# Turning finished attention segments on VectorE in 32x32 blocks, with output projections on the mixed layout

## The chip, the cores and the metric

The kernel runs on one core of a Trainium2 chip. The core has TensorE (PE in the profile; its weight loads are listed as PEld), VectorE (DVE), ScalarE (ACT), GpSimd (POOL) and SyncE (SP, which here only issues transfers), each with an instruction stream of its own; they wait for each other by semaphores. SBUF is the working memory of 128 partitions, PSUM holds the results of TensorE in eight banks of 128 x 512 fp32. The metric is the device time of one execution in microseconds.

## The reference, cut to what matters

Four layers over x of 2048 tokens and 512 features, alternating two kinds, each on the layer-normed input and added back to x:

```python
def _A_ref(x, wq, wk, wv, wo):            # layers 0 and 2
    H = 32; Dh = 16                       # 32 query heads, one shared key and value head
    q = (x @ wq).reshape(B, S, H, Dh) ... # to heads first
    k = x @ wk; v = x @ wv
    p = softmax(einsum("bhqd,bkd->bhqk", q, k) * Dh ** -0.5)
    o = einsum("bhqk,bkd->bhqd", p, v)
    return o.reshape(B, S, H * Dh) @ wo

def _B_ref(x, wqkv, wo):                  # layers 1 and 3: linear attention
    q, k, v = ...; phi = lambda t: where(t > 0, t + 1, exp(t)) + 1e-6
    kv = einsum("bhsd,bhse->bhde", phi(k), v); z = phi(k) summed over s
    o = (phi(q) @ kv) / (phi(q) . z + 1e-6)
    return o.reshape(B, S, D) @ wo

x = x + _A_ref(_layernorm(x), ...); x = x + _B_ref(_layernorm(x), ...)   # twice
```

## The kernel before, in words

The 2048 tokens are 16 tiles of 128. A Python planner (class `Planner`) plays the whole program through with a list of assumed durations, gives each operation to an engine when it is eligible, the engine free and its priority first, and writes down the order. The instruction streams are those orders, fixed when the program is built; the assumed durations (0.6 for a copy of 128x512, 0.12 for a transpose, ...) thus decide the order, though not the real time.

**Attention (layers 0 and 2, `run_a`).** A segment (`Seg`) is one query tile and one parity of heads: QT holds the queries of a tile as 128 partitions (four groups j of 32, two heads each) by four groups of 128 tokens, and the masked key array KM picks even or odd heads. A block is one key tile and one j: a score matmul with 32 rows (L1051) gives 128 keys x 512 columns in a PSUM bank. The exponential of a block is done by ScalarE for two or three banks at once (L1240, from `act_stream`), or by VectorE (L1344): it writes int16 bits, and GpSimd adds constants to four such blocks as 64-bit integers three times (L1386) to make three weighted shifts of it, so that a block done by VectorE is multiplied by the values four times (VW) instead of once (V). The results lie in W, 72 blocks of SBUF. `pv_try` sends value matmuls (L1105) in fours, one for each j, 32 columns wide, side by side in the array, all into bank 6 (ACC). Six banks hold scores; bank 7, and at times others, serve everything else from the pool `banks`. When TensorE would idle, `fill` adds matmuls with zero weights (L1150).

**The end of a segment.** `norms` takes the segments in turn. When all value matmuls of one are sent, VectorE copies ACC to SBUF as fp32 (`sacc`, L1407), which frees ACC for the next segment. Segments of the first tiles come in two or three parts over the keys; the first part is copied, later ones are added to it (L1409), and only the last is normalized. `norm` then acquires a bank, turns sacc by four fp32 transposes on TensorE (L1429), takes the reciprocal of the denominators, which are column 16 of each 32 (L1436), and multiplies (L1440) into Osb in bf16: tokens on partitions, features in the order of the heads.

**The output projection (`epilogue`).** Both parities done, Osb is turned to OT by a transposing DMA on SP (L794, tiles below 12), or by TensorE (L1468; L815 for tile 15). Four full matmuls with OT as weights and wo as moving data (L786) go to a bank, which VectorE adds to x (L1486). Tile 15, which ends the stage, goes through `proj2` (L829, L837) in two halves of 256 columns with x added by TensorE, followed at once by the next layer's statistics.

**Linear attention (layers 1 and 3, `run_b`)** is worked off beside the attention as far as its tiles are ready: projections (L786, L966), `phi` (ScalarE L1516, VectorE L1517 and L1519), sums over tokens. L1517 and the layer norm's scaling (L884) read and write SBUF only; the planner keeps them and GpSimd's L1386 apart in its own time (`port=True`). L936 makes the weighted values VW.

**Weights.** `late` loads wo, wqkv and wo2 on SP's queue once the keys of layer 0 are there.

Of the kernel before, what the change touches and what calls it, by code (L numbers as in the profile page):

```python
# [16 lines left out]
P = 128  # L17
# [533 lines left out]
def bass_interleave_layers__grouped_kv_mqa__linear_attn_block__prompt_kernel(  # L551
# [11 lines left out]
    pl = Planner(nc)  # L563
# [142 lines left out]
    def late():  # L706
        yield ("flag", ("K", 0, T - 1))
        pool_op(lambda e: e.memset(va[:].rearrange("p t (h c) -> p (t h) c", c=17)[:, :, DH:DH + 1], 1.0), [("va", i) for i in range(8)], dur=1.2, prio=5.0)
        dma(wo[:], A_wo.rearrange("(g r) c -> r g c", r=P), ["wo"], 3.0, 4.5)
        dma(wqkv[:], B_wqkv.rearrange("(ft f) c -> f ft c", f=P), ["wqkv"], 3.1, 9.5)  # L710
        dma(wo2[:], B_wo.rearrange("(g r) c -> r g c", r=P), ["wo2"], 3.2, 10.5)

# [110 lines left out]
        b1 = yield ("acq", banks, prio)  # L823
        return b0, b1

    def proj2(bs, lhs, rhs, t, key, prio):
# [4 lines left out]
        for h in range(2):  # L831
            hs = slice(h * 256, h * 256 + 256)

            def fn(e, h=h, hs=hs):
                ins = None
                for g in range(4):
                    ins = e.matmul(bank(bs[h], 256), lhsT=lhs(g), rhs=rhs(g, hs), start=False, stop=(g == 3))  # L837
                return ins
            op({PE: (0.45, fn)}, reads=key, writes=[B_(bs[h])], prio=prio, lat=0.2).cols = 1024
        os_ = []  # L840
        for h in range(2):
            hs = slice(h * 256, h * 256 + 256)
# [199 lines left out]
    def run_a(L):  # L1042
# [353 lines left out]
        def norms():  # L1396
            for sg in segs:
                pl.flag(("acc", L, sg.i))
                pl.at(pl.now, pv_kick)
                yield ("flag", ("pv", L, sg.i))  # L1400
                if sg.first and sg.last:
                    a_ = yield ("acq", as_pool, 0.0)
                    src, key = sacc[:, a_, :], ("sacc", a_)
                else:
                    a_, src, key = None, sacc[:, sg.unit, :], ("sacc", sg.unit)
                if sg.first:
                    o = op({DV: (0.6, lambda e, src=src: e.tensor_copy(src, bank(ACC)))}, writes=[B_(ACC), key], prio=0.0, lat=0.15)  # L1407
                else:
                    o = op({DV: (0.6, lambda e, src=src: e.tensor_tensor(out=src, in0=src, in1=bank(ACC), op=ALU.add))},  # L1409
                           writes=[B_(ACC), key], prio=0.0, lat=0.15)  # L1410
                if sg.last:
                    pl.process(norm(sg, src, key, a_))
                yield ("ops", [o])
            lin["a"] = False
            if L == 2 and LEND:
                lin["lent"] = True
                plain_give(banks, ACC)

        def norm(sg, src, key, a_):
            pr = 0.5  # L1420
            if sg.par == 0:
                oslot[sg.t] = yield ("acq", os_pool, 0.0)
                pl.flag(("oslot", L, sg.t))
            yield ("flag", ("oslot", L, sg.t))
            yield from until(key)
            b = yield ("acq", banks, pr)

            for c in range(4):
                o = op({PE: (0.12, lambda e, c=c: e.transpose(ps[:, b * 512 + c * P:b * 512 + (c + 1) * P], src[:, c * P:(c + 1) * P], identF[:]))},  # L1429
                       reads=[key, "identF"], writes=[B_(b)], prio=pr, lat=0.2)  # L1430
# [4 lines left out]
            rr = rden[:, r_, :].rearrange("p (c j) -> p c j", j=4)  # L1435
            op({DV: (0.17, lambda e: e.reciprocal(rr.unsqueeze(3), v4[:, :, :, DH:DH + 1]))},  # L1436
               writes=[B_(b), ("rden", r_)], prio=pr, lat=0.15)
            dst = Osb[:, oslot[sg.t], :].rearrange("p (g j r d) -> p r g j d", g=4, j=4, r=2)[:, sg.par]
            rb = rr.unsqueeze(3).to_broadcast([P, 4, 4, DH])
            o = op({DV: (0.33, lambda e: e.tensor_tensor(out=dst, in0=v4[:, :, :, 0:DH], in1=rb, op=ALU.mult))},  # L1440
                   reads=[("rden", r_)], writes=[B_(b), ("Osb", oslot[sg.t], sg.par)], prio=pr, lat=0.15)
            pl.give_after(banks, b, [o])
            yield ("ops", [o])
            pl.flag(("O", L, sg.t, sg.par))

        def epilogue(t):
# [29 lines left out]
                yield from until(("OT", m))  # L1476
            if t in ECRIT:
                bs = yield from acq2(pr)
                proj2(bs, lambda g: OT[:, m, g, :], lambda g, hs: wo[:, g, hs], t, [("OT", m), "wo"], pr)
# [499 lines left out]
```

## Time and profile before

| | |
|---|---|
| median of three timed runs | 1393.38 us (1393.33 to 1393.57) |
| profiled execution, its own time | 1391.23 us |
| its span | 1389.3 us |
| granted TensorE clock, mean | 0.999 |
| busy: TensorE, ScalarE, VectorE, GpSimd | 1344.2, 1347.3, 1216.5, 1033.0 us |
| exponentials on ScalarE (L1240) | 1332 instructions, 1287.5 us |
| exponentials on VectorE (L1344) | 1332 blocks, 868.8 us |
| copies of ACC (L1407) | 64, 43.6 us |
| transposes of sacc on TensorE (L1429) | 256, 46.0 us |
| scaling into Osb (L1440) | 64, 26.7 us |

How to read it: a row of a group names the source line, the engine, the operation, what it writes and reads by the program's names, the shapes and the count; then the busy time and the mean duration of one; then the idle time of the engine just before and what ended it. A wait row names the waiting engine and line, whom it waited for, the total, how often, the longest. A row of a stretch of time has the busy time of each engine with its instruction count, then the granted clock and the transfers. A timeline row has the start, the length, the engine and the operation. TensorE's busy time includes overlapped matmuls and filler, so its share alone says little.

### The profile page before, as it was taken

Reading aid. Unit: us, or ns where it says so; the run is one execution under the profiler, and the core shown is the slowest. Engines: PE = TensorE matmul, PEld = TensorE weight load, DVE = VectorE, ACT = ScalarE, POOL = GpSimd, SP = SyncE. Lnnn points to the kernel's source line nnn. Section 1 sums busy time; section 2 is a strip of 40 time slices with the busy share of each in tenths; the row PEclk is TensorE's granted clock in tenths of the full one; section 3 lists DMA queues with packets and bytes.
Section 4 is the critical chain, followed back from the end, with each engine's and each line's share of the span. In section 5 each row is a group of like instructions: output and inputs, shape, how many; then the busy total and the mean of one; then the engine's idle time right before and its main releaser. Section 6 shows DMA issues by size and latency. Waiting matters only on the chain.

```text
span 1389.3 us, 38426 instructions
## 1 busy us (share of the span) xinstructions
PE 1344.2 (97%) x15092; PEld 465.4 (33%) x15092; DVE 1216.5 (88%) x2184; ACT 1347.3 (97%) x1543; POOL 1033.0 (74%) x1031
## 2 busy tenths in 40 slices
PE   8999999999999999999999999999999999999998
PEld 5422222232222222233632333333333322223335
DVE  8889888898889988897889988988898899888977
ACT  8999999999999999999799999999999999999996
POOL 1489998778979998776005878867888799977770
PEclk9999999999999999999999999999999999999999
DMA  4300000000000000000021000000000000000001
GB/s 108 93 6 5 6 6 20 6 13 2 10 9 6 5 6 13 2 1 3 5 51 36 5 5 9 21 6 6 13 6 9 5 6 5 6 13 2 2 2 62
DMA packets 52465, 20.58 MB, mean 15 GB/s; under 512 B 46144, under 2 KB 51776, under 8 KB 52288
## 3 DMA queue, kind: packets, MB, share of 16 engines
q1 hardware_dynamic: 51232, 18.10, 5.7%
q8 instruction: 122, 2.00, 0.6%
q14 instruction: 55, 0.45, 0.1%
q10 hardware_dynamic: 1056, 0.03, 0.0%
HBM read 5.28 MB, written 2.10 MB: 5 GB/s over the span
## 4 chain that ended last, share of the span: by engine, by line
PE 52%; ACT 29%; DVE 9%; issue 7%; POOL 1%; DMA 1%; SPq 0%; ACTq 0%; DVEq 0%; POOLq 0%
ACT W L1240 28%; PE ps L1105 20%; PE ps L1051 17%; PE ps L786 6%; DVE W L1344 5%; PE ps L966 3%; PE ps L1429 2%; PE ps L1150 2%; POOL W L1386 1%; ACT phE L1516 1%; DVE phE L1517 1%; DVE sacc L1407 1%; DVE xn L884 1%; DMA x_sb<-in_A_x_dram 1%; DVE st L871 0%
## 5 line engine op out<-in xcount | busy, mean ns | idle before, releaser
L1240 ACT ACTIVATE W<-ps 128x1024 bf16<-128x1024 f32 (+1 forms) x1332 | 1287.5, 1157 | 11.5 <-PE ps L1051 8.4
L1386 POOL INT64_ADD W<-W x999 | 1027.4, 1041 | 314.7 <-DVE W L1344 156.8
L1344 DVE TENSOR_SCALAR W<-ps 128x512 int16<-128x512 f32 x1332 | 868.8, 683 | 121.8 <-PE ps L1051 106.5
L1105 PE MATMUL ps<-W,VW 128*32 128x512 bf16 x5328 | 562.4, 384 | 7.5 <-DVE sacc L1407 7.1
L1051 PE MATMUL ps<-QT,KM 32*128 32x512 bf16 x4096 | 520.7, 385 | 23.9 <-ACT W L1240 12.9
L1105 PE MATMUL ps<-W,V 128*32 128x512 bf16 x2764 | 447.7, 384 | 0.0
L1051 PEld LDWEIGHTS ps<-QT,KM 32*128 32x128 bf16 x4096 | 130.5, 91 | 508.0 <-ACT W L1240 444.6
L1105 PEld LDWEIGHTS ps<-W,VW 128*32 128x32 bf16 x5328 | 133.7, 94 | 177.6 <-issue 115.8
L1105 PEld LDWEIGHTS ps<-W,V 128*32 128x32 bf16 x2764 | 108.0, 94 | 71.2 <-issue 46.7
L786 PE MATMUL ps<-wqkv,xnT 128*128 128x512 bf16 (+1 forms) x272 | 76.1, 371 | 1.7 <-DVE sacc L1519 1.5
L1150 PE MATMUL ps<-QT,V 128*32 128x512 bf16 (+4 forms) x278 | 74.1, 333 | 0.9 <-DVE QT L780 0.8
L1516 ACT ACTIVATE phE<-ps 128x512 bf16<-128x512 f32 (+1 forms) x66 | 43.5, 663 | 6.8 <-PE ps L966 6.7
L1407 DVE COPY sacc<-ps 128x512 f32<-128x512 f32 x64 | 43.6, 681 | 6.0 <-PE ps L1105 5.9
L1429 PE MATMUL ps<-identF,sacc 128*128 128x128 f32 x256 | 46.0, 292 | 1.6 <-DVE sacc L1519 0.8
L871 DVE BATCH_NORM_STATS2 st<-x_sb 128x6 f32<-128x512 bf16 x60 | 40.5, 680 | 0.6 <-DMA x_sb<-in_A_x_dram 0.3
L884 DVE TENSOR_SCALAR xn<-x_sb,mv,rs 128x512 bf16<-128x512 bf16 x64 | 35.6, 571 | 2.2 <-ACT rs L862 2.0
L966 PE MATMUL ps<-xnT,wqkv 128*128 128x128 bf16 x512 | 37.4, 220 | 0.0
L1517 DVE TENSOR_SCALAR phE<-phE 128x512 bf16<-128x512 bf16 (+1 forms) x66 | 33.2, 506 | 4.5 <-ACT phE L1516 4.1
L786 PE MATMUL ps<-wo,OT 128*128 128x512 bf16 x120 | 36.0, 384 | 0.9 <-DVE QT L1519 0.5
L966 PE MATMUL ps<-xnT,wq 128*128 128x128 bf16 x464 | 35.2, 220 | 0.0
L1429 PEld LDWEIGHTS ps<-identF,sacc 128*128 128x128 f32 x256 | 27.6, 142 | 19.9 <-issue 14.3
L1150 PEld LDWEIGHTS ps<-QT,V 128*32 128x32 bf16 x278 | 22.7, 95 | 29.7 <-issue 15.6
(140 smaller groups left out, 599.0 us busy)
## 6 DMA issues: line engine op xcount, KB each, us to landing
out_dram<-x_sb SPq DMA_DIRECT2D x16, 128.0 KB, 1.7
x_sb<-in_A_x_dram SPq DMA_DIRECT2D x6, 256.0 KB, 5.4
wqkv<-in_B_wqkv_dram SPq DMA_DIRECT2D x1, 1536.0 KB, 7.9
xnT<-xn SPq DMA_TRANSPOSE x46, 2.5
x_sb<-in_A_x_dram SPq DMA_DIRECT2D x4, 128.0 KB, 2.2
wq<-in_A_wq_dram SPq DMA_DIRECT2D x1, 512.0 KB, 4.2
wo<-in_A_wo_dram SPq DMA_DIRECT2D x1, 512.0 KB, 4.1
wo<-in_B_wo_dram SPq DMA_DIRECT2D x1, 512.0 KB, 8.8
```

Of the source, the lines that this page charges most:

```text
L786: return e.matmul(dst, lhsT=l, rhs=r, start=(k == 0), stop=(k == len(pairs) - 1))
L884: op({DV: (0.325, lambda e: e.tensor_scalar(out=xn[:, i, :], in0=x_sb[:, t, :], scalar1=mv[:, t, 0:1], scalar2=rs[:, t:t + 1], op0=ALU.sub ...
L966: ins = e.matmul(dst[:, g * P:(g + 1) * P], lhsT=lhs(g, k), rhs=rhs(k), start=(k == 0), stop=(k == FT - 1))
L1051: return e.matmul(bank(b), lhsT=KM[r, sg.par, kt * P:(kt + 1) * P], rhs=QT[r, sg.t, :], start=True, stop=True)
L1105: ins = e.matmul(ps[32 * j:32 * j + 32, ACC * 512:(ACC + 1) * 512], lhsT=V[:, kt, :] if w is None else VW[:, kt, w, :], rhs=ap, start=(k = ...
L1150: o = op({PE: (n / 2400.0, lambda e: e.matmul(ps[32 * j:32 * j + 32, b * 512:b * 512 + n], lhsT=V0[:], rhs=QT[:, sg.t, 0:n], start=st, sto ...
L1240: ex = op({AC: (EXO + 0.4267 * n, lambda e, n=n, s_=s_, p_=p_: e.activation(ws_(p_), ps[:, s_ * 512:(s_ + n) * 512], ACTF.Exp, scale=EXPSC ...
L1344: o = op({DV: (0.602, lambda e: e.tensor_scalar(out=dst.bitcast(I16), in0=bank(b), scalar1=VB, scalar2=VLO, op0=ALU.add, op1=ALU.max))}, w ...
L1386: o = op({PO: (512 * m * PSR + PSO, lambda e, g_=g_, f_=f_: e.int64_add(ws_(g_).bitcast(I64), ws_(f_).bitcast(I64), step))}, reads=wk_(f_) ...
L1407: o = op({DV: (0.6, lambda e, src=src: e.tensor_copy(src, bank(ACC)))}, writes=[B_(ACC), key], prio=0.0, lat=0.15)
L1429: o = op({PE: (0.12, lambda e, c=c: e.transpose(ps[:, b * 512 + c * P:b * 512 + (c + 1) * P], src[:, c * P:(c + 1) * P], identF[:]))}, rea ...
L1516: op({AC: (0.07 + n / 1200.0, lambda e: e.activation(phE[:, i, 0:n], bank(b, n), ACTF.Exp))}, reads=[B_(b)], writes=[("phE", i)], prio=pr ...
```

## The change

VectorE has a transpose that turns each 32x32 block of a 128x512 array on its own. A segment that comes in one part is turned by it straight out of ACC into sacc, in place of the copy; one that comes in parts is copied and added as before, and its sum is turned from SBUF into one of the two `as_pool` slots of sacc. TensorE's transposes and the bank they needed go. The result has a mixed layout: on partition 32j + q lies token q of each of the four 32-token blocks b of a tile, for the heads of group j. Reciprocal and scaling read it in SBUF, and Osb has its columns ordered by b, then by head within j. After the same transposing step as before, OT holds for each b the features of all four j side by side, 32 columns for each j. The output projection therefore takes, for each j, four matmuls of 32 weight columns, one for each b, each into its own 32 partitions of the bank (`quarters`), with wo's rows regrouped by j; wo is loaded as four transfers into 32 partitions each. `proj2` gets the same form for tile 15 (`col=True`), after its full matmul with x. The assumed duration of the transpose is 0.62 (TRD), and the projection's steps are marked for the planner with the mode of the value matmuls. All orders are planned anew. Its core:

```diff
+TRD = 0.62
+WO_ = [("wo", g) for g in range(4)]
@@ late
-        dma(wo[:], A_wo.rearrange("(g r) c -> r g c", r=P), ["wo"], 3.0, 4.5)
+        wv_ = A_wo.rearrange("(g j q) c -> g q j c", g=4, j=4)
+        for g in range(4):
+            dma(wo[32 * g:32 * g + 32, :, :], wv_[g], [("wo", g)], 3.0, 4.5)
@@
+    def quarters(e, b, cs, l, r, start, stop):
+        ins = None
+        for q in range(4):
+            ins = e.matmul(ps[32 * q:32 * q + 32, b * 512 + cs.start:b * 512 + cs.stop], lhsT=l[:, q, :], rhs=r, start=start, stop=stop)
+        return ins
@@ proj2
                 for g in range(4):
-                    ins = e.matmul(bank(bs[h], 256), lhsT=lhs(g), rhs=rhs(g, hs), start=False, stop=(g == 3))
+                    if col:
+                        ins = quarters(e, bs[h], slice(0, 256), lhs(g), rhs(g, hs), False, g == 3)
+                    else:
+                        ins = e.matmul(bank(bs[h], 256), lhsT=lhs(g), rhs=rhs(g, hs), start=False, stop=(g == 3))
...
@@ norms
                 if sg.first and sg.last:
                     a_ = yield ("acq", as_pool, 0.0)
                     src, key = sacc[:, a_, :], ("sacc", a_)
-                else:
-                    a_, src, key = None, sacc[:, sg.unit, :], ("sacc", sg.unit)
-                if sg.first:
+                    o = op({DV: (TRD, lambda e, src=src: e.transpose(src, bank(ACC)))}, writes=[B_(ACC), key], prio=0.0, lat=0.15)
+                elif sg.first:
+                    src, key = sacc[:, sg.unit, :], ("sacc", sg.unit)
                     o = op({DV: (0.6, lambda e, src=src: e.tensor_copy(src, bank(ACC)))}, writes=[B_(ACC), key], prio=0.0, lat=0.15)
...
@@ norm
-            b = yield ("acq", banks, pr)
-
-            for c in range(4):
-                o = op({PE: (0.12, lambda e, c=c: e.transpose(ps[:, b * 512 + c * P:b * 512 + (c + 1) * P], src[:, c * P:(c + 1) * P], identF[:]))},
-                       reads=[key, "identF"], writes=[B_(b)], prio=pr, lat=0.2)
-            if a_ is not None:
-                pl.give_after(as_pool, a_, [o])
+            if a_ is None:
+                a_ = yield ("acq", as_pool, pr)
+                op({DV: (TRD, lambda e: e.transpose(sacc[:, a_, :], src))}, reads=[key], writes=[("sacc", a_)], prio=pr, lat=0.15)
+            key = ("sacc", a_)
             r_ = sg.i % 2
-            v4 = bank(b).rearrange("p (c j d) -> p c j d", c=4, j=4)
+            v4 = sacc[:, a_, :].rearrange("p (c b q) -> p c b q", c=4, b=4)
...
-            dst = Osb[:, oslot[sg.t], :].rearrange("p (g j r d) -> p r g j d", g=4, j=4, r=2)[:, sg.par]
+            dst = Osb[:, oslot[sg.t], :].rearrange("p (b c r d) -> p r c b d", b=4, c=4, r=2)[:, sg.par]
...
@@ epilogue
-            o = mm(bank(b), [(OT[:, m, g, :], wo[:, g, :]) for g in range(4)], [("OT", m), "wo"], b, pr, 0.9)
+            for j in range(4):
+                o = op({PE: (0.222, lambda e, j=j: quarters(e, b, slice(0, 512), OT[:, m, :, 32 * j:32 * j + 32], wo[:, j, :], j == 0, j == 3))},
+                       reads=[("OT", m)] + WO_, writes=[B_(b)], prio=pr, lat=0.2, mode="col")
+                o.cols = 512
```

More of the change, by code (lines that the diff above doesn't have):

```diff
@@ L836, in fn @@
                 for g in range(4):
-                    ins = e.matmul(bank(bs[h], 256), lhsT=lhs(g), rhs=rhs(g, hs), start=False, stop=(g == 3))
+                    if col:
+                        ins = quarters(e, bs[h], slice(0, 256), lhs(g), rhs(g, hs), False, g == 3)
+                    else:
+                        ins = e.matmul(bank(bs[h], 256), lhsT=lhs(g), rhs=rhs(g, hs), start=False, stop=(g == 3))
                 return ins
-            op({PE: (0.45, fn)}, reads=key, writes=[B_(bs[h])], prio=prio, lat=0.2).cols = 1024
+            op({PE: (0.45, fn)}, reads=key, writes=[B_(bs[h])], prio=prio, lat=0.2, mode="col" if col else "full").cols = 1024
         os_ = []
@@ L1411, in norms @@
                 if sg.last:
-                    pl.process(norm(sg, src, key, a_))
+                    pl.process(norm(sg, src, key, a_ if sg.first else None))
                 yield ("ops", [o])
```

13 lines of the change are left out of this document (7 added, 6 removed).

## The prediction

> **What bounds the kernel now.** I read the page first (engine totals, the chain that ended last, the transfers), then who waited for whom, then totals by stretches of time, and last the timeline at the places that the change touches. From the page:
>
> ```profile
> span 1389.3 us, 38426 instructions
> ...
> PE 1344.2 (97%) x15092; PEld 465.4 (33%) x15092; DVE 1216.5 (88%) x2184; ACT 1347.3 (97%) x1543; POOL 1033.0 (74%) x1031
> ...
> PE 52%; ACT 29%; DVE 9%; issue 7%; POOL 1%; DMA 1%; SPq 0%; ACTq 0%; DVEq 0%; POOLq 0%
> ...
> wo<-in_A_wo_dram SPq DMA_DIRECT2D x1, 512.0 KB, 4.1
> ```
>
> TensorE and ScalarE are both at 97% and the chain prefers TensorE. The waits say which of the two is really scarce:
>
> ```profile
> PEld ps L1051 <- ACT W L1240: 444.6, 1085, 1.0
> PEld ps L1051 <- DVE W L1344: 19.2, 52, 0.5
> PE ps L1105 <- DVE sacc L1407: 7.1, 15, 0.8
> ACT W L1240 <- PE ps L1051: 8.4, 19, 1.8
> ACT W L1240 <- PE ps L1105: 1.8, 4, 0.6
> ```
>
> The score matmuls (L1051) stood ready for 444.6 us until an exponential (L1240) gave their PSUM banks back; the other way round the exponentials waited for TensorE 8.4 + 1.8 = 10.2 us in the whole run. VectorE's exponentials (L1344) were the last to free a bank 52 times against ScalarE's 1085. So in the two attention stages ScalarE sets the pace:
>
> ```profile
> 60.00:630.00 570.00, 555.20 (x6258) 167.35 (x6255) 503.55 (x858) 567.31 (x625) 496.78 (x485) 1.00 0.04 7
> 660.00:690.00 30.00, 29.92 (x377) 21.81 (x374) 25.70 (x75) 22.80 (x50) 0.00 (x0) 1.00 0.01 2
> 740.00:1330.00 590.00, 569.52 (x6442) 183.40 (x6440) 525.01 (x892) 581.19 (x645) 478.25 (x466) 1.00 0.04 9
> ```
>
> The columns are PE, PEld, DVE, ACT, POOL. ScalarE (fourth) was idle 2.7 us of 570 in the first attention stage and 8.8 us of 590 in the second. Between the stages (second row) all engines are partly idle and a chain of latencies decides; the end of the run is of that kind too. A change can thus act in three ways: through the amount of ScalarE work, through the few microseconds in which ScalarE waits, and through the chains behind the last segment of each stage.
>
> **The change part by part.** The groups that it touches:
>
> ```profile
> L1240 ACT ACTIVATE W<-ps 128x1024 bf16<-128x1024 f32 x1228 | 1157.8, 1126 | 9.8 <-PE ps L1051 8.4
> L1240 ACT ACTIVATE W<-ps 128x1536 bf16<-128x1536 f32 x102 | 151.0, 1534 | 1.8 <-PE ps L1105 1.8
> L1429 PE MATMUL ps<-identF,sacc 128*128 128x128 f32 x256 | 46.0, 292 | 1.6 <-DVE sacc L1519 0.8 <-DVE QT L1519 0.6
> L1407 DVE COPY sacc<-ps 128x512 f32<-128x512 f32 x64 | 43.6, 681 | 6.0 <-PE ps L1105 5.9
> L1440 DVE TENSOR_TENSOR Osb<-ps,rden 128x256 bf16<-128x256 f32 x64 | 26.7, 417 | 0.8
> L728 DVE STREAM_TRANSPOSE rampT<-ramp 128x32 f32<-128x32 f32 x1 | 0.2, 211 | 0.0
> ```
>
> *1. The planner deals the exponentials out anew.* Counting the instruction streams of both kernels: ScalarE's exponentials go from 1228 of two blocks, 102 of three and 2 of one (2764 blocks) to 1260, 82 and none (2766 blocks); VectorE's from 1332 to 1330. Two blocks more cost 2 x (1534 - 1126) ns = 0.8 us, ten instructions more cost 10 x (1157.8/1228 - 2 x 0.408) = 10 x 0.127 = 1.3 us: +2.1 us. By the busy column instead: 32 x 0.943 - 20 x 1.480 = +0.6, less two single blocks of at least 0.408, so -0.2 us. I take the middle, +1.0, with both ends kept. All of it is on the engine that paces.
>
> *2. The fp32 transposes on TensorE go* (64 x 4, L1429). One set inside attention:
>
> ```profile
> 143.53 0.66 PE L1429 MATMUL ps<-identF,sacc 128*128 128x128 f32 x4
> 144.12 0.61 PE L1105 MATMUL ps<-W,VW 128*32 128x512 bf16 x8
> 144.57 1.45 ACT L1240 ACTIVATE W<-ps 128x1536 bf16<-128x1536 f32 x1 [0.55 <-PE ps L1105]
> ```
>
> It held TensorE from 143.53 to 144.12, 0.59 us with the change of array mode; 64 of them are 38 us. Here the value matmuls behind it came late, and an exponential that needed their weight blocks freed waited 0.55 us. That is the kind of wait that the change can remove. It is not worth 38 us, because TensorE is not short: the new stream has zero-weight filler matmuls (L1150) of 168,576 columns instead of 109,696, 115 slots of 512 more. A slot is 0.22 us, the distance of these starts:
>
> ```profile
> 655.39 0.39 PE L1105 MATMUL ps<-W,VW 128*32 128x512 bf16 x4
> 655.61 0.39 PE L1105 MATMUL ps<-W,V 128*32 128x512 bf16 x4
> ```
>
> So 25 us of the 38 go straight to filler. The gain is bounded by the 10.2 us that ScalarE waits for TensorE at all; the other end is 0. Of the four waits behind L1105 (1.8 us) this one is 0.55, about a third; most waits name score matmuls that have other work ahead of them. I take a quarter: -2.5 us. The norm also no longer needs a PSUM bank, which the same few banks' other users gain; the counts in part 1 show that the planner made no more VectorE blocks of it, so 0.
>
> *3. VectorE turns the accumulator instead of copying it.* For 52 segments a transpose replaces a copy one for one, on the path accumulator, next segment's value matmuls (these waited 7.1 us for L1407). The 12 segments assembled in parts keep their copies and additions and get a transpose from SBUF besides. The trace has one such transpose, 211 ns for 32 columns. Ends: 0.681 us, a copy of the same 512 columns, and 16 x 0.211 = 3.4 us if blocks do not overlap. I take 0.70, next to the copy: 211 ns for 32 columns is the size of a fixed cost, and 512 columns at the copy's pace are the bulk. The far end, 2.7 us for each of 52 turnovers, would lie far outside any range below; I give it next to nothing. So the 52 cost 1.0 us of VectorE and nothing at the end; the 12 cost 12 x 0.70 = 8.4 us of VectorE.
> On the same price the Trainium skill, "VectorE: DVE Perf Modes", section "The three transpose paths", gives 311 ns for 128x128 in bf16; as an estimate with the row's 211 ns that is 33 ns for a further block and 0.71 us for sixteen, which would leave the sum as it is.
>
> *4. Reciprocal and scaling now read SBUF.* The scaling (L1440) had one input in PSUM and one in SBUF; now both lie in SBUF. What that means beside a busy GpSimd is seen by other lines. In order L1440, L936 (the only tensor-by-tensor product of attention with both inputs in SBUF) and L1517:
>
> ```profile
> 60.00:630.00 570.00, 12.50 (x30) 1.00 0.04 7
> 740.00:1330.00 590.00, 12.53 (x30) 1.00 0.04 9
> ```
> ```profile
> 20.00:60.00 40.00, 2.93 (x12) 1.00 0.41 103
> 740.00:1330.00 590.00, 4.68 (x6) 1.00 0.04 9
> ```
> ```profile
> 60.00:630.00 570.00, 7.32 (x18) 1.00 0.04 7
> 660.00:690.00 30.00, 2.85 (x11) 1.00 0.01 2
> 740.00:1330.00 590.00, 17.64 (x24) 1.00 0.04 9
> ```
>
> L1440 takes 0.417 us in both stages, whatever GpSimd does. L936 goes from 0.244 us, ahead of GpSimd's work, to 0.780 beside it: 0.54 more. L1517 goes from 0.259 with GpSimd idle to 0.407 and 0.735. So some VectorE instructions on SBUF wait for GpSimd, and the scaling becomes one of the kind that L936 is. Ends: 0, and 64 x 0.54 = 34 us of VectorE time. I take 0.54 x 30 = 16 us in the second stage (L936's own), and in the first 10 us, between L1517's 0.148 x 30 = 4 and 16: 26 us.
> The rule behind this is in the Trainium skill, "SBUF — State Buffer", section "Who interferes with whom": a VectorE instruction with two SBUF inputs contends with a GpSimd instruction that reads SBUF, and the second to start blocks until the first is done. The trace's L936 agrees; without that rule the term for the scaling would be 0, and the sum 3.9 us lower.
>
> What of the 26 + 8.4 + 1.0 = 35 us reaches ScalarE? VectorE has room: 503.55 of 570 and 525.01 of 590 busy. Lower end 0. Upper end: the second stage has more of such waiting (L1517 11.4 us and L936 3.2 us, against 2.7) and more idle ScalarE (8.8 against 2.7 us); if all of that came from it, 6.1/11.9 = 0.51. I take 0.15, much nearer 0, since a score matmul found VectorE last only once in 21: +5.3 us. Queued behind a stalled scaling are the next L1344, hence its weight block, GpSimd's three shifts of it, and the next score matmul into its bank. GpSimd is held up in turn, at most 64 x 0.42 = 27 us, hidden by its own idle 73 and 112 us; without that cover late weight blocks would hold the value matmuls.
>
> *5. The output projections in four column tiles.* 30 tiles get 4 x 4 matmuls of 32 columns instead of 4 full ones, on the same queue places.
>
> ```profile
> 1349.34 1.04 PE L786 MATMUL ps<-wqkv,xnT 128*128 128x512 bf16 x4
> ```
> ```profile
> 656.05 0.69 DVE L1407 COPY sacc<-ps 128x512 f32<-128x512 f32 x1 [1.13 <-PE ps L1105]
> 656.83 0.62 PE L1429 MATMUL ps<-identF,sacc 128*128 128x128 f32 x4
> 657.49 0.26 DVE L1436 RECIPROCAL rden<-ps 128x16 f32<-128x16 f32 x1 [0.75 <-PE ps L1429]
> 657.87 0.42 DVE L1440 TENSOR_TENSOR Osb<-ps,rden 128x256 bf16<-128x256 f32 x1
> 658.40 0.39 PE L815 MATMUL ps<-ident,Osb 128*128 128x128 bf16 x4
> ```
>
> Four concurrent quarter matmuls start every 0.22 us (655.39, 655.61), four full ones run at (1.04 - 0.38)/3 = 0.22 us each: no change, and beside value matmuls a mode change less. Taken as 0; without TensorE's slack, 480 more weight loads would be the risk.
>
> *6. The end of each attention stage.* From the last value matmuls (655.61) to L815 it is 2.79 us: copy, transposes, reciprocal, scaling. GpSimd is silent by then. New: 655.61 + 0.44 to the transpose, 0.70, then 0.26 and 0.42 with some 0.1 us between each: L815 at about 657.8, 0.6 earlier. In the new stream 32 projection matmuls stand between instead of 36 and the four transposes, so TensorE is there too. The projection of tile 15 follows as 32 quarter matmuls of 256 columns and costs two mode changes, 0.1 each. So -0.4 us per stage end, twice: -0.8; ends -2 and +1.
>
> *7. Weights.* wo comes as four transfers into 32 partitions each, three more issues on SP ahead of those of wqkv and wo2.
>
> ```profile
> 39.83 0.58 SPq L693 DMA_DIRECT2D wo<-in_A_wo_dram  x1
> ...
> L786 PE MATMUL ps<-wo,OT x120: 379/379/390, 89.2 to 1328.8; 128*128 128x512 bf16 x120
> ```
>
> Issued at 39.83, landed in 4.1 us, first read at 89.2: the 45 us between hide three issues of some 0.6 us and slower landings. 0.
>
> **Sum.** +1.0 - 2.5 + 5.3 - 0.8 = +3.0 us. The profiled execution took 1391.23 us (span 1389.3 and 1.9 around it), so it would take 1394.2; the median of the three timed runs is 1393.38, 2.15 higher, so 1396.4. That is +0.21%, just beyond 0.2% (2.8 us), about what a measurement of this kernel can tell from no change.
>
> **Rivals.**
> *TensorE's relief wins (faster).* One mechanism: waits of ScalarE behind TensorE go. For it: the row at 144.57, and 13 us of TensorE time really freed. Against it: only 10.2 us exist. With six tenths of them gone and 0.03 of VectorE's 35 us passed on: 1.0 - 6.1 + 1.1 - 0.8 = -4.8, 1388.6. It decides from where what is relieved exceeds what VectorE passes on by 3 us.
> *They cancel.* Passing on 0.05 to 0.1 instead of 0.15 gives +1.8 - 2.5 + 1.0 - 0.8 to +3.5 - 2.3, so -0.5 to +1.2: about 1393.7.
> *Contention passes through (clearly slower).* At 0.51 of 35 us: 1.0 - 2.5 + 17.9 - 0.8 = +15.6, 1409. For it: the busier second stage has the idle ScalarE. Against: 52 against 1085.
> *The transpose takes two cycles per column.* Then 0.53 us more for each of 52 turnovers, 28 us on the value path; the score matmuls' lead over the exponentials covers most; a quarter is +7, 1403.
>
> **How the numbers follow.** Forecast, a little slower (1396.2 to 1401): 0.30. Cancelled: 0.29. Faster: 0.29. Contention or a slow transpose: 0.12. So faster 0.29, same 0.29, slower 0.42. The range from 1388 to 1406 leaves out the far halves of the faster case and of the last one, less than 0.2.
>
> **What would show it.** L1429's row gone and filler up by about 25 us of slots; the transpose at 0.70 us; the scaling at 0.8 to 0.95 us in 740 to 1330 and 0.42 at the stage ends; ScalarE's idle time in the two stages up by 2 to 4 us; L815 about 2.2 us behind the last value matmuls. Wrong would be: scaling still 0.42 (no contention), a transpose above 1 us, or ScalarE's idle time falling below 8 us.

## The result, and the profile after

The changed kernel takes 1406.28 us (median of six runs, 1403.75 to 1408.56), the kernel before beside it 1392.09 (1390.69 to 1393.57): a ratio of 1.0102, 95% interval 1.0088 to 1.0116. It is 14.2 us slower; the forecast was 1396.4, 3.0 us slower, with a range from 1388 to 1406. The profiled execution took 1408.56 us.

From the page of the kernel after: span, busy times, chain.

```profile
span 1406.8 us, 39103 instructions
...
PE 1348.7 (96%) x15392; PEld 454.6 (32%) x15392; DVE 1249.9 (89%) x2195; ACT 1353.6 (96%) x1552; POOL 1039.0 (74%) x1031
...
PE 59%; DVE 18%; ACT 17%; issue 6%; POOL 1%; ACTq 0%; DVEq 0%
```

VectorE has 33 us more work and twice its former share of the chain (9% before). The groups of the change, by shape:

```profile
L1451 DVE TENSOR_TENSOR Osb<-sacc,rden 128x256 bf16<-128x256 f32 x64 | 62.6, 978 | 0.2
L1417 DVE STREAM_TRANSPOSE sacc<-ps 128x512 f32<-128x512 f32 x52 | 36.8, 707 | 4.2 <-PE ps L1118 4.2
L1442 DVE STREAM_TRANSPOSE sacc<-sacc 128x512 f32<-128x512 f32 x12 | 8.4, 701 | 0.0
```

The transposes take what was forecast. The scaling rose from 417 to 978 ns. The two attention stages (PE, PEld, DVE, ACT, POOL), and the scaling alone in them and at the first stage's end:

```profile
60.00:630.00 570.00, 545.36 (x6270) 159.75 (x6266) 515.66 (x844) 556.29 (x614) 493.49 (x479) 0.99 0.04 7
740.00:1330.00 590.00, 568.05 (x6515) 176.82 (x6513) 533.66 (x902) 581.42 (x656) 473.00 (x456) 1.00 0.05 10
```
```profile
60.00:630.00 570.00, 32.88 (x29) 0.99 0.04 7
670.00:694.00 24.00, 0.42 (x1) 1.00 0.01 2
740.00:1330.00 590.00, 24.80 (x29) 1.00 0.05 10
```

ScalarE, which sets the pace, is idle 13.7 us of the first 570 (2.7 before) and 8.6 of the 590 (8.8 before). The scaling is 1.13 us on average in the first stage, 0.86 in the second, 0.42 where GpSimd is silent. Cut at the first and last attention exponential of each layer on ScalarE, the span divides so (us):

| | head | first stage | between | second stage | tail |
|---|---|---|---|---|---|
| before | 9.5 | 645.8 | 24.7 | 672.2 | 37.2 |
| after | 11.0 | 659.5 | 23.6 | 676.8 | 35.9 |

The loss is in the attention stages. The waits tell through whom, after and then before (where ScalarE's was 8.4 us, 19 times, longest 1.8):

```profile
ACT W L1253 <- PE ps L1064: 22.0, 41, 2.6
PE ps L1064 <- DVE W L1357: 17.6, 27, 2.8
```
```profile
PE ps L1051 <- DVE W L1344: 4.1, 8, 1.6
```

There are more waits, and longer ones. The timeline shows one of them, then the same stretch with the granted clock as the column after GpSimd's:

```profile
227.56 4.10 POOL L1399 INT64_ADD W<-W  x4
...
228.32 3.62 DVE L1451 TENSOR_TENSOR Osb<-sacc,rden 128x256 bf16<-128x256 f32 x1
...
231.86 2.47 DVE L1357 TENSOR_SCALAR W<-ps 128x512 int16<-128x512 f32 x4
...
232.68 0.61 PE L1064 MATMUL ps<-QT,KM 32*128 32x512 bf16 x3 [2.69 <-DVE W L1357]
233.23 2.05 POOL L1399 INT64_ADD W<-W  x2 [1.57 <-DVE W L1357]
233.34 1.02 ACT L1253 ACTIVATE W<-ps 128x1024 bf16<-128x1024 f32 x1 [2.62 <-PE ps L1064]
```
```profile
225.00:231.00 6.00, 4.57 (x53) 1.26 (x51) 6.00 (x8) 5.72 (x7) 6.00 (x7) 1.00 0.00 0
232.00:238.00 6.00, 5.32 (x41) 1.03 (x41) 4.31 (x7) 3.07 (x3) 3.38 (x4) 0.50 0.11 25
239.00:245.00 6.00, 6.00 (x85) 1.62 (x81) 4.29 (x8) 5.91 (x8) 4.66 (x5) 1.00 0.00 0
```

One scaling stands for 3.62 us beside four additions of GpSimd that run one after the other, and ends 0.28 us after the last of them (231.66). The VectorE exponentials behind it are late, so the PSUM banks that they would have freed are late, TensorE idles 2.69 us, ScalarE 2.62, and GpSimd itself 1.57. Then TensorE runs at half clock for 6.8 us, and ScalarE is busy only 3.07 of the next 6 us.

Five of the 64 scalings took 3.1 to 4.0 us (starts 146.96, 228.32, 506.38, 547.46 and 1106.96), four of them in the first stage; the other 59 took at most 1.3 us, 0.76 on average. No scaling took over 0.43 us before. The five stood through three or four additions each. Of the others 39 waited (those over 0.5 us), each for one addition, and in 12 of these GpSimd's next addition was just as close behind; why the five didn't get in between is open. Not every long stop reaches the other engines: after four of the five TensorE idled 2.2 to 2.8 us, while behind the longest (547.46, 4.03 us) neither TensorE nor ScalarE shows an idle stretch above 0.41 us in the next 12 us.

### The profile page after: what moved, and what is told of

Same layout as the page of the kernel before. It is cut to its first block, busy times and chain, and to the rows that moved or that the text cites. A ratio compares the mean times of both kernels' runs of the same rounds, so it can differ in the third digit from the quotient of the medians.

```text
span 1406.8 us, 39103 instructions
## 1 busy us (share of the span) xinstructions
PE 1348.7 (96%) x15392; PEld 454.6 (32%) x15392; DVE 1249.9 (89%) x2195; ACT 1353.6 (96%) x1552; POOL 1039.0 (74%) x1031
## 4 chain that ended last, share of the span: by engine, by line
PE 59%; DVE 18%; ACT 17%; issue 6%; POOL 1%; ACTq 0%; DVEq 0%
PE ps L1118 25%; PE ps L1064 19%; ACT W L1253 16%; DVE W L1357 9%; PE ps L790 5%; PE ps L1163 3%; PE ps L979 3%; PE ps L833 2%; DVE Osb L1451 1%; DVE sacc L1417 1%; DVE st L884 1%; DVE phE L1531 1%; DVE xn L897 1%; POOL W L1399 1%; ACT phE L1530 1%
## 5 line engine op out<-in xcount | busy, mean ns | idle before, releaser
L1118 PE MATMUL ps<-W,VW 128*32 128x512 bf16 x5320 | 577.3, 386 | 9.6 <-DVE sacc L1417 7.9
L1064 PE MATMUL ps<-QT,KM 32*128 32x512 bf16 x4096 | 526.5, 386 | 36.1 <-DVE W L1357 17.6
L1118 PE MATMUL ps<-W,V 128*32 128x512 bf16 x2766 | 473.8, 387 | 0.0
L1163 PE MATMUL ps<-QT,V 128*32 128x512 bf16 (+5 forms) x438 | 115.8, 329 | 0.6 <-DVE QT L784 0.4
L1451 DVE TENSOR_TENSOR Osb<-sacc,rden 128x256 bf16<-128x256 f32 x64 | 62.6, 978 | 0.2
L1163 PEld LDWEIGHTS ps<-QT,V 128*32 128x32 bf16 x438 | 36.0, 95 | 41.3 <-issue 23.3
L833 PE MATMUL ps<-wo,OT 128*32 128x512 bf16 (+1 forms) x544 | 45.3, 370 | 0.1
L1417 DVE STREAM_TRANSPOSE sacc<-ps 128x512 f32<-128x512 f32 x52 | 36.8, 707 | 4.2 <-PE ps L1118 4.2
L979 PEld LDWEIGHTS ps<-xnT,wqkv 128*128 128x128 bf16 x512 | 29.4, 98 | 9.1 <-issue 6.7
```

Of the source, the lines that this page charges most:

```text
L833: ins = e.matmul(ps[32 * q:32 * q + 32, b * 512 + cs.start:b * 512 + cs.stop], lhsT=l[:, q, :], rhs=r, start=start, stop=stop)
L979: ins = e.matmul(dst[:, g * P:(g + 1) * P], lhsT=lhs(g, k), rhs=rhs(k), start=(k == 0), stop=(k == FT - 1))
L1064: return e.matmul(bank(b), lhsT=KM[r, sg.par, kt * P:(kt + 1) * P], rhs=QT[r, sg.t, :], start=True, stop=True)
L1118: ins = e.matmul(ps[32 * j:32 * j + 32, ACC * 512:(ACC + 1) * 512], lhsT=V[:, kt, :] if w is None else VW[:, kt, w, :], rhs=ap, start=(k = ...
L1163: o = op({PE: (n / 2400.0, lambda e: e.matmul(ps[32 * j:32 * j + 32, b * 512:b * 512 + n], lhsT=V0[:], rhs=QT[:, sg.t, 0:n], start=st, sto ...
```

## The experiments

Times are medians, against the kernel before on the same chip (1390.9 to 1391.5 us in the five groups of runs). In runs on the changed kernel's own orders only the instructions named differ.

**Is it contention at all?** First the changed kernel with an instruction of one SBUF input in the scaling's place:

```diff
-            o = op({DV: (0.33, lambda e: e.tensor_tensor(out=dst, in0=v4[:, :, :, 0:DH], in1=rb, op=ALU.mult))},
+            o = op({DV: (0.33, lambda e: e.transpose(dumT[:], sacc[:, a_, 0:256]))},
```

> The changed kernel, all orders kept, with each scaling replaced by a block transpose of 256 columns from SBUF to an unused SBUF buffer, which has one input; the normalization is left out, and the projections work on a constant Osb. Theory 1: no such instruction waits for GpSimd (0.45 us each), and the time falls to 1390 to 1396 us with at most one halving of the clock. Theory 2: it stays at 1402 us or more.

Measured 1386.24 us (1386.2 to 1387.2), ratio 0.9964 [0.9951, 0.9977]. Group and wait:

```profile
L1452 DVE STREAM_TRANSPOSE dumT<-sacc 128x256 f32<-128x256 f32 x64 | 27.6, 431 | 0.2
```
```profile
ACT W L1254 <- PE ps L1065: 6.5, 21, 0.7
```

Nearly the unstalled length of the scaling, no stall (the longest took 0.45 us), and 20.0 us less than the changed kernel, on the side of theory 1 and below its range: the contention costs 20.0 us, and all else in the change is a gain of 5.2 us. Then the contention alone, in the kernel before and its orders: a second product at the same 64 places, once with both inputs in SBUF, once from PSUM (`v4`) as a control.

```diff
-            o = op({DV: (0.33, lambda e: e.tensor_tensor(out=dst, in0=v4[:, :, :, 0:DH], in1=rb, op=ALU.mult))},
+            o = op({DV: (0.33, lambda e: (e.tensor_tensor(out=dd, in0=d4[:, :, :, 0:DH], in1=rb, op=ALU.mult),
+                                          e.tensor_tensor(out=dst, in0=v4[:, :, :, 0:DH], in1=rb, op=ALU.mult))[1])},
```

> The kernel before, all orders kept, with one more instruction ahead of each scaling: a product of the same 256 columns with both inputs in SBUF, whose result nobody reads. Theory 1: the added product takes 0.42 us where GpSimd is idle and 0.9 to 1.0 us on the mean in attention, with a few of 3 us and more; 8 to 15 us slower than before, 1400 to 1407 us, and more than one halving of the clock. Theory 2: no more than its own 0.42 us times 64 on an engine that is not the bound, so the same as the next kernel within 2 us.

> The control to the run before: the kernel before, all orders kept, with the scaling done twice, both times with its first input in PSUM, the second result going nowhere. 27 us more of VectorE work without contention. Theory 1: 0 to 3 us slower, 1391 to 1395 us. Theory 2: the same as the kernel with the SBUF product within 2 us.

```profile
L1444 DVE TENSOR_TENSOR dumO<-dumA,rden 128x256 bf16<-128x256 f32 x64 | 51.1, 799 | 0.8
```
```profile
L1444 DVE TENSOR_TENSOR dumO<-ps,rden 128x256 bf16<-128x256 f32 x64 | 26.8, 418 | 0.8
```

From SBUF 1406.72 us (ratio 1.0123 [1.0099, 1.0147]), from PSUM 1393.79 (1.0017 [1.0008, 1.0027]). The same product costs 12.9 us more for the place of one input, with 24 us of stalls. Plain VectorE time passed on 2.3 of 26.8 us, the stalls half of theirs. ScalarE's waits, SBUF and then PSUM:

```profile
ACT W L1242 <- PE ps L1053: 16.2, 38, 0.8
```
```profile
ACT W L1242 <- PE ps L1053: 8.7, 20, 1.6
```

The time is as theory 1 had it, but not by the way it expected: no product took over 1.30 us here, and the granted clock was 1.00 throughout. So stalls cost much even where none is long and the clock never halves.

**Does the amount of VectorE time explain that?** A third product from PSUM gives the kernel before as much further time as the stalled one took:

> Before, in its own orders, with the scaling done three times from PSUM (two further products of 128x256 into spare SBUF at each of the 64 places): about 53.6 us of further VectorE time, as much as the product with two SBUF inputs took with its stalls (51.1 us, +15.2 us in time), but never stopped by GpSimd. Theory 'the stop itself': uncontended VectorE time passes on as the first 26.8 us did (+2.3 us, 0.09), so +4.5 to +6.5: 1396 to 1398.5. Rival 'the amount': any 51 us more on VectorE at these places cost about 15 us, because the slack is used up past some length: 1404 to 1408.

Measured 1401.50 us (ratio 1.0069 [1.0056, 1.0083]): +10.0, against +15.2 for the product with its stalls. Both theories missed; the second 26.8 us cost 7.7 where the first had cost 2.3. VectorE's room is used up by degrees, and a good part of what the short stalls cost is the amount of VectorE time. In the changed kernel, the same question with a plain 0.97 us at each place:

```diff
-            o = op({DV: (0.33, lambda e: e.tensor_tensor(out=dst, in0=v4[:, :, :, 0:DH], in1=rb, op=ALU.mult))},
+            o = op({DV: (0.33, lambda e: (e.transpose(dumU[:], sacc[:, a_, 0:384]), e.transpose(dumT[:], sacc[:, a_, 0:256]))[1])},
```

> The changed kernel with the scaling replaced by two block transposes from SBUF, of 384 and of 256 columns (normalization left out), at the same places of the same orders: some 0.57 + 0.43 us, about the 0.98 us that the scaling took with its stalls, but always the same length and never stopped by GpSimd. The transpose of 256 alone took 1386.24 us, the stalled scaling 1406.28. Theory 'the amount': 36 us more on VectorE at these places cost what the stalls cost, whatever makes them: 1402 to 1407. Rival 'the stops': a plain 0.98 us costs what plain time cost in the kernel before (10.0 us for 53.6 us of it, 0.19): 1391 to 1396, and what is left to 1406 belongs to the uneven length of the stalls, the few of 3 to 4 us above all.

```profile
L1453 DVE STREAM_TRANSPOSE dumU<-sacc 128x384 f32<-128x384 f32 x64 | 36.2, 566 | 0.2
L1453 DVE STREAM_TRANSPOSE dumT<-sacc 128x256 f32<-128x256 f32 x64 | 25.8, 404 | 0.0
```

Measured 1397.83 us (1396.8 to 1399.0), between the two again: 62.0 us evenly spread cost 11.6 more than 27.6, against 20.0 for the 62.6 us of stalled scalings. So 8.4 us belong to something that equal pieces don't have. Two runs on the same orders asked whether it is the uneven length: plain work of the lengths that the stalls had, at the places where they had them, and the five long ones alone, without the `else` branch. `k` counts the 64 places; the reductions take 2.7 to 3.7 us:

```diff
+    LONG = {5: 308, 9: 372, 23: 368, 25: 424, 50: 368}
...
+                n = LONG.get(k, 0)
+                if n:
+                    e.tensor_reduce(out=dumR[:, 0:1], in_=sacc[:, a_, 0:n].unsqueeze(1).to_broadcast([P, 8, n]), op=ALU.add, axis=mybir.AxisListType.XY)
+                else:
+                    e.transpose(dumU[:], sacc[:, a_, 0:192])
+                return e.transpose(dumT[:], sacc[:, a_, 0:256])
```

> The changed kernel with the scaling replaced by plain VectorE work of the lengths that the stalled scalings had (normalization left out), same orders: at five of the 64 places, those at which the scaling took 3.1 to 4.0 us, a reduction of 2.6 to 3.5 us and a block transpose of 256 columns; at the other 59 two block transposes of 192 and 256 columns, about 0.76 us. Theory 'uneven lengths': the five long stops are what is missing, 1403 to 1408. Rival 'something else of contention': no more than evenly spread time of the same sum, 1396 to 1399.

> The same with the five long stops alone: a reduction of 2.6 to 3.5 us ahead of the block transpose of 256 columns at five places, nothing added at the other 59 (1386.24 us without the five). Theory 'uneven lengths': each long stop costs 2 us or more, 1395 to 1400. Rival 'amount alone': 15.5 us at 0.32, or 1390 to 1392.

All lengths: 1409.26 us (1408.8 to 1410.0). The five alone: 1403.75 (1402.4 to 1404.7), 17.5 us for 16.0 us of reductions. Both lie above the ranges of both theories, on the side of 'uneven lengths'. One of them in the timeline, without any contention:

```profile
230.56 3.23 DVE L1461 TENSOR_REDUCE dumR<-sacc 128x1 f32<-128x2976 f32 x1
...
233.71 0.43 DVE L1462 STREAM_TRANSPOSE dumT<-sacc 128x256 f32<-128x256 f32 x1
234.07 2.44 DVE L1362 TENSOR_SCALAR W<-ps 128x512 int16<-128x512 f32 x4
...
234.87 0.39 PE L1069 MATMUL ps<-QT,KM 32*128 32x512 bf16 x3 [2.63 <-DVE W L1362]
235.30 1.02 ACT L1258 ACTIVATE W<-ps 128x1024 bf16<-128x1024 f32 x1 [2.35 <-PE ps L1069]
```
```profile
235.50:238.80 3.30, 3.30 (x31) 0.52 (x27) 2.57 (x5) 2.12 (x3) 2.36 (x3) 0.50 0.14 32
```

The same row of waits as in the changed kernel, and the half clock behind it. So in these orders the long stops make up most of the imitated loss: the five cost 3.5 us each on average (the longest again leaves no idle above 0.4 us behind it), the other 59 together 5.5 by difference (1409.26 - 1403.75). The plain imitation is 3.0 us above what it imitates; why is open. It says nothing of the kernel before's orders, where the stalls of the second product cost 12.9 us without one long stop.

**Can the planner be told?** The changed kernel with assumed 0.23 and 0.98 for reciprocal and scaling:

> The changed kernel with the planner's assumed durations of reciprocal and scaling set to what they took (0.23 and 0.98), so that it deals the work out knowing VectorE's real time. Theory 'contention is the cost and stays': scaling still 0.85 to 1.05 us on average, 1398 to 1410. Rival 'the cost was that the orders did not know of the stalls': 1392 or less.

```profile
L1451 DVE TENSOR_TENSOR Osb<-sacc,rden 128x256 bf16<-128x256 f32 x64 | 45.5, 711 | 0.3
```

1400.78 us (ratio 1.0080 [1.0065, 1.0095]). The scaling is shorter than expected in these orders, and the kernel still 9.8 us behind. Here no scaling took over 1.29 us, and the clock did not halve within the stages: long stops come with a deal, and without them the kernel is still slower. How much of the 9.8 us is the stalls' and how much the deal's, this run doesn't show.

**Without the second SBUF input.** The reciprocals go to a PSUM bank, acquired for reciprocal and scaling; all is dealt out anew:

```diff
-            r_ = sg.i % 2
+            b = yield ("acq", banks, pr)
...
-            rr = rden[:, r_, :].rearrange("p (c b) -> p c b", b=4)
+            rr = bank(b, 16).rearrange("p (c b) -> p c b", b=4)
...
+            pl.give_after(banks, b, [o])
```

> The changed kernel, with the reciprocals of the denominators written to a PSUM bank instead of SBUF, so that the scaling has one SBUF input and one PSUM input; everything else of the change stays, the orders are planned anew. Theory 1 (the scaling with two SBUF inputs waits for GpSimd, in a few cases through three or four of its instructions; VectorE, TensorE and ScalarE stop behind it and the TensorE clock halves after such a stop): the scaling takes 0.42 us everywhere, no VectorE instruction over 1.5 us, ScalarE's idle time in the first attention stage falls from 14 us to 3 to 6 us, 1388 to 1394 us in all. Theory 2 (the new orders themselves, with ten more exponentials on ScalarE and the column tiles, cost the time): 1402 us or more.

Measured 1396.39 us (1.0036 [1.0023, 1.0049]): no stall, but a miss. ScalarE's idle time in the first stage is 4.2 us, as expected, and the two stages (table below) are 6.7 us shorter than before; the tail is 48.8 us instead of 37. In its timeline two waits of ScalarE stand there (5.61 and 4.10 us), both in the last layer's linear attention, which this deal orders differently. Hence the same with the assumed durations nearer the measured ones (0.23 and 0.42; then 0.24 and 0.42), and the kernel before with that edit as a control:

> The changed kernel with the reciprocals in a PSUM bank again, as in the run that took 1396.39 us, and with the durations that the planner assumes for reciprocal and scaling set near the measured ones (0.23 and 0.42 instead of 0.17 and 0.33), so that the work is dealt out anew. Theory 'contention was the loss, and the first version lost its gain to a badly dealt last stage': scaling 0.41 us, first stage 643 to 650, second 664 to 672, tail 34 to 38 instead of 48.8: 1384 to 1390. Rival 'the bank held for the reciprocals costs what contention did': tail mended and total still 1392 or more, with more idle ScalarE behind TensorE in the second stage.

> The version at 1386.26 us (reciprocals in a PSUM bank) with the planner's assumed duration of the reciprocal 0.24 instead of 0.23, so that all is dealt out once more. Theory 'without contention the change is a few us faster than before, give or take the deal': scaling 0.41 us, 1383 to 1392. Rival 'the 1386 was luck of one deal': above 1392.

> Before, with only the planner's assumed durations of reciprocal and scaling raised from 0.17 and 0.33 to 0.23 and 0.42, the edit that came along in the version at 1386.26 us. Theory 'the 1386 is due to the change without its contention': no gain here, 1390 to 1397, by the luck of the deal. Rival 'any plan with truer durations wins': 1388 or less.

```profile
L1451 DVE TENSOR_TENSOR Osb<-sacc,ps 128x256 bf16<-128x256 f32 x64 | 26.1, 407 | 0.4
```

| | median, us | ratio | first stage | second stage | both | tail |
|---|---|---|---|---|---|---|
| before | | | 645.8 | 672.2 | 1318.0 | 37.2 |
| before, 0.23 and 0.42 | 1395.12 | 1.0033 [1.0021, 1.0046] | 644.1 | 671.3 | 1315.4 | 43.9 |
| PSUM, 0.17 and 0.33 | 1396.39 | 1.0036 [1.0023, 1.0049] | 646.5 | 664.8 | 1311.3 | 48.8 |
| PSUM, 0.23 and 0.42 | 1386.26 | 0.9958 [0.9946, 0.9971] | 643.4 | 669.6 | 1313.0 | 36.0 |
| PSUM, 0.24 and 0.42 | 1390.26 | 0.9999 [0.9989, 1.0010] | 640.8 | 668.8 | 1309.6 | 40.8 |

All three came out as their first theories expected. In the three PSUM deals the two attention stages together are 5.0 to 8.4 us shorter than in the kernel before, and still 2.4 to 5.8 shorter than in the kernel before dealt anew; the tail varies by 13 us with the deal and decides the total. The version at 1386.26 us is the fastest full kernel here, 5.3 us ahead of the kernel before; how much of that a further deal would keep is open, since the third one is level with it.

**The scaling on GpSimd.**

```diff
-            o = op({DV: (0.33, lambda e: e.tensor_tensor(out=dst, in0=v4[:, :, :, 0:DH], in1=rb, op=ALU.mult))},
+            o = op({PO: (0.9, lambda e: e.tensor_tensor(out=dst, in0=v4[:, :, :, 0:DH], in1=rb, op=ALU.mult))},
```

> The changed kernel with the scaling given to GpSimd (assumed 0.9 us) and dealt out anew. Theory 'contention between the two engines': on GpSimd it comes one after the other with the 64-bit additions, so VectorE no longer stops for it; VectorE's own groups keep the lengths they have without contention, and the time is 1386 to 1394 if GpSimd's 64 x 0.9 = 58 us find room in its idle 326 us. Rival 'GpSimd becomes late': the value matmuls wait longer for the weight blocks behind it, or the end of each stage grows by 1 us or more: 1396 or more.

2170.01 us: neither theory is near. GpSimd's timeline and waits:

```profile
119.58 1.04 POOL L1399 INT64_ADD W<-W  x1
127.75 0.61 POOL L1451 TENSOR_TENSOR Osb<-sacc,rden 128x256 bf16<-128x256 f32 x1 [7.13 <-issue]
134.23 5.45 POOL L1399 INT64_ADD W<-W  x5 [5.87 <-issue]
```
```profile
POOL W L1399 <- issue: 365.8, 61, 6.6
POOL Osb L1451 <- issue: 350.3, 49, 7.8
```

The product itself takes 0.61 us, less than assumed. But each change from one kind of instruction to the other is an idle of some 7.1 or 6.0 us. In 110 of the 127 changes GpSimd waits for nothing that the profile shows, 716 us in all, close to the 779 that it costs.

**The two steps on TensorE.** On the kernel without normalization (1386.24 us), full 128-column projections instead of column tiles, at the same places:

```diff
-        for q in range(4):
-            ins = e.matmul(ps[32 * q:32 * q + 32, b * 512 + cs.start:b * 512 + cs.stop], lhsT=l[:, q, :], rhs=r, start=start, stop=stop)
+        return e.matmul(ps[:, b * 512 + cs.start:b * 512 + cs.stop], lhsT=l, rhs=r, start=start, stop=stop)
```

> The same kernel without normalization (1386.24 us), with each four 32-column projection matmuls replaced by one full matmul of 128 columns at the same places in the orders (wrong layout, so other numbers come out). Theory 'column tiles cost nothing': 1385.5 to 1387.0. Rival 'the 1632 further matmuls and weight loads cost': at least 2 us faster, below 1384.5.

1390.14 us (1388.7 to 1391.5), 3.9 more. The weight loads, full and then in column tiles:

```profile
L833 PEld LDWEIGHTS ps<-wo,OT 128*128 128x128 bf16 x136 | 11.2, 96 | 24.3 <-issue 21.6 <-DVE OT L785 0.9 <-DVE W L1356 0.7
```
```profile
L834 PEld LDWEIGHTS ps<-wo,OT 128*32 128x32 bf16 x544 | 12.5, 95 | 11.3 <-issue 8.4 <-DVE QT L785 0.5 <-DVE OT L785 0.2
```

Both theories missed, having left out that side: behind value matmuls of 32 columns a full matmul starts 0.32 us after the one before it, a column tile 0.22, and the weight loads' idle time is 13 us more in sum. I read this as a change of array mode. (The 1632 further matmuls of the expectation should be 408, 544 less 136.) It says nothing of four full ones in a row, as the kernel before had them.

Then TensorE time was put back, as matmuls of zero columns ahead of a segment's first value matmul:

```diff
+                if not any(sg.emitted):
+                    for c in range(11):
+                        e.matmul(ps[:, ACC * 512:ACC * 512 + P], lhsT=zz[:], rhs=zz[:], start=True, stop=True)
```

> The changed kernel with the scaling replaced by a block transpose of 256 columns (normalization left out, as in the run that took 1386.24 us), and with 11 matmuls of 128 zero columns put ahead of the first value matmul of each segment: 64 x 0.59 us = 38 us on TensorE, what the transposes taken from it had held. Theory 'TensorE's relief': the -5.2 us against before are the relief, at least the -2.5 of the sum: 1388.5 to 1391.5. Rival 'the new plan': the relief is worth nothing, the new orders are: 1385.5 to 1387.

1446.64 us, +60.4. The run was mis-sized: the matmuls fell into all 92 parts of segments, not 64, at 0.72 us a time, 66 us. So once more, nine of them in the 64 normalized segments, with the filler shortened:

> The changed kernel with the scaling replaced by a block transpose of 256 columns (normalization left out, 1386.24 us), with 9 matmuls of 128 zero columns ahead of the first value matmul of the 64 normalized segments, some 0.59 us each and 38 us in all, and the zero-weight filler shortened from 168,576 to 99,392 columns, 30 us: TensorE has about the kernel before's amount of work again. Theory of the sum (relief worth 2.5 us): 1388 to 1390. Rival 'all of the 5.2 us is relief': 1391 to 1394. Rival 'none of it': 1385 to 1387. Above 1396: what counts is the place at the accumulator's turnover, not the amount.

```profile
ACT W L1257 <- PE ps L1065: 31.9, 81, 1.3
```

1422.60 us (1420.2 to 1425.0): +36 for 39 us, though 29 us of filler were gone (115.6 to 86.8 us busy). At the turnover of the accumulator, TensorE time was paid nearly in full in these two runs, and filler elsewhere did not pay it back. The transposes of the kernel before stood at other places, so this is no price for them.

## Why the prediction was wrong

**Step 1 (new deal, +1.0).** The amount was no loss: in the changed kernel's orders without contention (1386.24 us) ScalarE's exponentials are busy 1286.9 us against 1287.5 before. But the three deals of the version with PSUM gave 1386 to 1396 us for the same work, with the tail between 36 and 49; the step counted ScalarE's instructions and had no term for that.

**Steps 2 and 6 (-2.5 and -0.8).** Without contention the kernel is 5.2 us faster than before, where the sum without its 26 us of stalls is -0.9. Step 6 was right in sign: between the stages and in the tail the changed kernel gained 1.1 and 1.3 us, more than the 0.4 each; from the last value matmuls to L819 (L815 before) it is 2.07 us (670.75 to 672.82) where 2.2 was forecast. Step 2 is not shown by itself: without contention ScalarE's idle time before its exponentials fell from 11.5 to 6.9 us, but how that divides between TensorE's relief and the deal is open.

**Step 3 (0.70 us a transpose).** Held: 0.707 from PSUM, 0.701 from SBUF. The rival of two cycles per column is out.

**Step 4 (26 us of stalls, 0.15 passed on, +5.3) failed**, in the sizes. The mechanism was the one named: both inputs in SBUF, beside a busy GpSimd. By the Trainium skill, "SBUF — State Buffer", section "Who interferes with whom", such an instruction contends, and one with at most one SBUF input, outside the two-port modes, doesn't: the trace agrees, with 0.978 us for the product and 0.431 for the transpose at the same places. By its rule the second to start blocks until the first is done; 39 of the 44 stalled scalings agree, but five stood through three or four additions, 3.1 to 4.0 us, and the measurement decides.

Two sizes were wrong. The sum of stalls was 36 us: 12.7 in the second stage (24.80 - 29 x 0.417) where 16 was forecast, but 20.8 in the first (32.88 - 29 x 0.417) where the row of L1517 had led me to 10. Of the 36 the five long ones make 15.8 (17.9 - 5 x 0.417), which the step had no term for; the 20 of the other 59 are less than the 26 forecast. A mean of 0.54 us from L936 (none of which took over 1.21 us, and two of the six had not waited at all, at 0.28) said nothing of the longest stall.

And 20.0 of the 36 reached the time, 0.56, above even the upper end of 0.51. The argument for 0.15 was that a score matmul found VectorE last only once in 21. That count tells how often VectorE is late in the kernel before; it doesn't tell what further VectorE time does once the room is used. In the changed kernel's orders even plain equal pieces passed on 0.34 (11.6 of 34.4 us), and the five long reductions more than their length (17.5 for 16.0). In the kernel before, stalls of which none was long passed on 0.53. So a low share was wrong with and without long stops. Of the stop of 3.62 us, 2.62 us reached ScalarE, and the halved clock came on top.

**Step 5 (0).** Nothing in the trace speaks against it; in these orders column tiles are the cheaper form, by 3.9 us.

**Step 7 (0).** Held: the four parts of wo landed in a median of 2.6 us each.

Of the rivals, "contention passes through" (1409) is what happened, with more stall than it reckoned with and a gain elsewhere; it shared a chance of 0.12 with the slow transpose. "TensorE's relief wins" describes the kernel with the contention taken out.

## What to carry to other kernels

When a change gives a VectorE instruction a second SBUF input beside a busy GpSimd, don't price the stalls by a low share read from the kernel before. Ask for two things: how much VectorE time the stalls add, since each further piece costs more as the room is used up, and how long the longest stop can be, at most a whole unbroken run of GpSimd's queue, against the slack of what is queued behind. Keeping one input in PSUM took the stall away in every version tried. And where a planner deals all orders anew, expect some microseconds either way from the deal, and compare stage by stage before a total is put down to the edit.

## What the runs showed of the hardware

- A VectorE product of two SBUF inputs can lose to several GpSimd instructions in a row: 3.62 us beside four additions of some 1.05 us each, ended 0.28 us after GpSimd paused. This happened in 5 of 44 stalls of the changed kernel, and in none of the 47 of the second product in the kernel before.
- Four of the five stops of VectorE left TensorE idle for 2.2 to 2.8 us, and three were followed by a granted clock of 0.50 for 3.4 or 6.8 us (after 228.32, 506.38 and 1106.96). The five plain reductions alone did the same, three times of five. The kernel before has one such stretch within its stages too (1229.8, 3.4 us), behind an idle of TensorE of 1.64 us.
- GpSimd paid 5.7 to 7.8 us at nearly each change between 64-bit additions and a product. The Trainium skill, "GPSIMD Engine Reference", section "2.1 Instruction dispatch", states some 6 us without a visible instruction for the first call of a freshly loaded kernel; the size agrees, but here it came at every alternation.
- The block transpose of fp32 on VectorE took 0.43 us for 256 columns, 0.57 for 384 and 0.70 for 512, and never stalled beside GpSimd.
